# A written order for the early part of a fused attention and MLP kernel, and a later assumed crossbar landing

## Chip, cores and metric

One core of a Trainium2 chip. The metric is the device time of one launch, in microseconds (us). Of the 113 runs of the kernel before beside the experiments, 110 were fast, and 101 of these lie within 0.3% of the median of their rounds; three fell in a slower state (182.75 to 183.62 us, at a granted clock of 0.987 to 0.991), and only fast runs are compared here. A ratio is the mean time of one kernel's fast runs over that of the other's of the same rounds, so it is not quite the ratio of the medians that are quoted beside it.

## The reference

```python
# q, k, v, alpha: (4, 8, 768, 48)  (batch, heads, tokens, head_dim)
for t in range(S):
    state = alpha[:, :, t, :, None] * state + np.einsum('bhd,bhe->bhde', k[:, :, t], v[:, :, t])
    y[:, :, t] = np.einsum('bhd,bhde->bhe', q[:, :, t], state)
x = y.transpose(0, 2, 1, 3).reshape(3072, 384)
h = x @ w_in                                        # (384, 2048)
g = 0.5 * h * (1 + tanh(c * (h + 0.044715 * h**3)))
out = g @ w_out                                     # (2048, 384)
```

## The kernel before

The kernel splits the tokens in six chunks of 128 and each chunk in two pairs of batches: twelve pairs. For a pair it takes logarithms of alpha (`ln`), sums them on TensorE (`cum`, tile `cum`), exponentiates (`b`, `binv`), scales q and k (`qp`, `kp`), transposes them (`t`, tile `qkT`), multiplies and masks them (`attn`, tile `at`; `mask`, tile `atm`), multiplies with v (`y`, tile `yps`), and carries the state (`kv`, `st`). Layer 1 (`l1`, tile `hT`), GELU and layer 2 (`l2`, tile `acc`) follow. Early pairs are transposed on TensorE, the eighth pair and later ones by DMA (ten `DMA_TRANSPOSE` of q and k in the trace, from 97.42 us on), called the crossbar here after the kernel's `xbar`.

The trace shows instructions of an engine in the order in which they are emitted: in that of the changed kernel ScalarE's first 30 instructions, from 0.73 to 20.67 us, stand in the order of its list (`FIRST` below). A scheduler in Python picks that order when the program is built: it plays the tasks through with fixed costs and takes the best candidate at each step. It also puts "idle" products on zeros into gaps of TensorE, to keep the array busy. The parts that matter here, cut:

```python
W = dict(..., landed=2200, xbar_qk=1500, xbar_x=1000, late_x=2500, ..., cold=380, fill=216, zero=1100)

class Scheduler:
    def order(self):
        ...
        while any(left.values()):
            best = None
            for e in LAT:                       # each engine: the ready task that may start first
                ...
            at, e, t = best
            if e == "PE" and self.fill and at < self.until and at - free[e] > 300:
                g = given("ff")
                n = int((at - max(free[e], g if g is not None else at) - 60) * 0.95 // W["fill"])
                if not free[e]:                 # the first gap: the array is slow
                    n = int((at - W["zero"]) // W["cold"])
                if n > 0:
                    ...                         # n idle products
            put(t, at, e)
            ...

    # GpSimd asks for loads in this order; a "gate" is a copy that waits for a tile
    LOADS = ('gatea 0 1', 'v0', 'gateqp 0 1', 'in 0', 'v1', 'in 1', 'in 2', 'in 3', 'out 0', ...)
```

## Time and profile before

| | median us | runs |
|---|---|---|
| before, at the time of the prediction | 180.68 | 3 |
| before, with the runs beside the changed kernel | 180.76 (180.13 to 181.17) | 6 |

The prediction below shows the busy shares, the table by stretch and the waits. What it doesn't show is the start, which turned out to matter. The timeline of TensorE of the kernel before (columns: start, length, engine, line, operation, tiles, shape, count, and in brackets the idle time just before and what ended it):

```profile
1.19 2.74 PE L225 MATMUL idle<-zero 128*128 128x512 bf16 x6 [1.19 <-DVE half L801]
4.33 1.09 PE L282 MATMUL cum<-la,ut_blk 128*128 128x384 f16 x7 [0.40 <-ACT la L295]
5.36 0.82 PE L282 MATMUL cum<-la,ut_blk 128*128 128x384 f16 x7
8.21 0.40 PE L425 MATMUL at<-qkT 64*128 64x128 bf16 x8
17.61 0.40 PE L425 MATMUL at<-qkT 64*128 64x128 bf16 x8
31.82 2.76 PE L527 MATMUL acc<-w_out,gT 128*128 128x384 bf16 x16
```

Six idle products run while alpha is on its way. In the start one idle product takes about 0.43 us (six take 2.74 us here, five take 2.31 in the changed kernel below), twice the 0.22 us of a later one. The first group of seven `cum` products takes 1.09 us and the second, which is the same work, 0.82: the array reaches full speed during the first one (0.82 is also what the groups at 12.24 and 13.37 us take). The two `at` lines are the first attention product of the first and of the second pair; the last line is the start of layer 2.

### The profile page before, as it was taken

How to read it: one execution, taken by the hardware profiler on the slowest of the kernel's cores; microseconds unless marked ns; L12 is line 12 of the kernel's file. 1: busy time of each engine (PE TensorE's matmuls, PEld its weight loads, DVE VectorE, ACT ScalarE, POOL GpSimd, SP SyncE). 2: the span in 40 equal slices, each digit the busy share in tenths (PEclk: the TensorE clock that was granted, in tenths of full speed). 3: DMA queues.
4: the chain of work that ended last, by engine and by line, in shares of the span. 5: the costliest groups of instructions: out<-in, count | busy, mean ns of one | idle time of the engine just before them, and what ended most of it. 6: DMA issues, size and time to landing. Idle time of an engine off the chain costs nothing.

```text
span 178.9 us, 4418 instructions
## 1 busy us (share of the span) xinstructions
PE 171.5 (96%) x1835; PEld 135.0 (75%) x1838; DVE 95.2 (53%) x187; ACT 131.3 (73%) x216; POOL 58.0 (32%) x64
## 2 busy tenths in 40 slices
PE   6979899999999999999999989999999999999992
PEld 2547699666896897797698679688697697786972
DVE  6669751054967894596499779195436405000000
ACT  4669778984898668858788948987988984481831
POOL 2496347986627766566520000000000000000000
PEclk9999999999999999999999999999999999999999
DMA  4999999999999999999998970362270360401102
GB/s 124 269 273 217 208 246 234 229 210 207 227 313 214 221 266 213 185 262 211 201 251 196 159 183 13 68 168 63 44 190 22 88 162 4 117 15 45 47 2 86
DMA packets 48901, 28.86 MB, mean 161 GB/s; under 512 B 37489, under 2 KB 45297, under 8 KB 48881
## 3 DMA queue, kind: packets, MB, share of 16 engines
q0 software_dynamic: 26464, 17.70, 59.5%
q1 hardware_dynamic: 22416, 10.88, 23.8%
q8 instruction: 14, 0.23, 0.6%
q14 instruction: 7, 0.05, 0.1%
HBM read 25.17 MB, written 4.72 MB: 167 GB/s over the span
## 4 chain that ended last, share of the span: by engine, by line
PE 88%; DMA 8%; DVE 1%; ACT 1%; SPq 0%; issue 0%; POOL 0%
PE hT L508 35%; PE acc L527 33%; PE at L425 4%; DMA v<-in_v_dram 3%; PE qkT_ps L364 3%; PE yps L482 3%; DMA qkT<-kp 3%; PE kv L442 2%; PE yps L479 2%; PE cum L314 2%; DMA a<-in_alpha_dram 2%; PE xT_ps L496 1%; PE idle L225 1%; PE cum L282 1%; PE cum L316 1%; PE k_ps L390 1%
## 5 line engine op out<-in xcount | busy, mean ns | idle before, releaser
L527 PE MATMUL acc<-w_out,gT 128*128 128x384 bf16 (+1 forms) x400 | 69.1, 319 | 0.0
L508 PE MATMUL hT<-xT,w_in 128*128 128x256 bf16 x576 | 69.0, 273 | 0.0
L514 ACT ACTIVATE gT<-hT 128x512 bf16<-128x512 f32 x96 | 56.8, 597 | 16.7 <-PE hT L508 13.1
L508 PEld LDWEIGHTS <-w_in 128*128 128x128 bf16 x576 | 61.1, 113 | 1.2
L527 PEld LDWEIGHTS <-gT 128*128 128x128 bf16 x400 | 36.6, 97 | 19.1
L432 DVE TENSOR_TENSOR atm<-at,ut 128x512 bf16<-128x512 f32 x48 | 30.2, 683 | 15.5 <-PE at L425 15.4
L354 DVE TENSOR_TENSOR qp<-q,b 128x768 bf16<-128x768 f32 (+1 forms) x15 | 11.9, 796 | 22.6 <-ACT b L343 14.4
L539 ACT COPY ot<-acc 128x384 f32<-128x384 f32 (+1 forms) x18 | 8.3, 460 | 14.1 <-PE acc L527 11.9
L244 POOL DMA_DIRECT2D k<-in_k_dram x11 | 12.2, 1107 | 8.6 <-DVE stmp L464 3.2
L244 POOL DMA_DIRECT2D q<-in_q_dram x11 | 12.2, 1108 | 7.2 <-DVE qp L354 1.6
L244 POOL DMA_DIRECT2D a<-in_alpha_dram x11 | 12.3, 1114 | 5.4 <-DMA w_in<-in_moe_w_in_dram 1.4
L244 POOL DMA_DIRECT2D vb<-in_v_dram x11 | 12.1, 1103 | 4.5 <-PE hT L508 1.3
L343 ACT ACTIVATE b<-cum 128x768 bf16<-128x768 f32 (+1 forms) x15 | 10.3, 684 | 2.7 <-PE cum L316 1.5
L216 ACT ACT_TABLE_LOAD x9 | 11.5, 1283 | 0.9 <-PEq L832 0.7
L354 DVE TENSOR_TENSOR kp<-k,binv 128x768 bf16<-128x768 f32 (+1 forms) x15 | 11.9, 792 | 0.0
L514 ACT ACT_TABLE_LOAD x9 | 11.5, 1283 | 0.2
L489 DVE CAST x<-yps 128x384 bf16<-128x384 f32 x11 | 6.1, 558 | 8.6 <-PE yps L482 5.6
L343 ACT ACTIVATE binv<-cum 128x768 bf16<-128x768 f32 (+1 forms) x15 | 10.2, 678 | 0.0
L464 DVE TENSOR_TENSOR stmp<-kv,st 128x384 f32<-128x384 f32 x16 | 8.8, 552 | 1.8 <-PE kv L442 1.8
L489 ACT CAST x<-yps 128x384 bf16<-128x384 f32 x13 | 6.2, 476 | 4.8 <-PE yps L482 4.8
L482 PE MATMUL yps<-vb,atm 128*128 128x48 bf16 x192 | 8.7, 183 | 0.8 <-ACT vb L325 0.8
L467 DVE TENSOR_TENSOR st<-stmp,ends 128x384 bf16<-128x384 f32 x16 | 8.9, 558 | 0.6
(63 smaller groups left out, 157.9 us busy)
## 6 DMA issues: line engine op xcount, KB each, us to landing
out_dram<-ot SPq DMA_DIRECT2D x23, 192.0 KB, 3.8
a<-in_alpha_dram POOLq DMA_DIRECT2D x9, 384.0 KB, 11.9
q<-in_q_dram POOLq DMA_DIRECT2D x9, 384.0 KB, 11.5
k<-in_k_dram POOLq DMA_DIRECT2D x9, 384.0 KB, 11.4
vb<-in_v_dram POOLq DMA_DIRECT2D x9, 192.0 KB, 11.6
w_in<-in_moe_w_in_dram POOLq DMA_DIRECT2D x4, 384.0 KB, 10.0
w_out<-in_moe_w_out_dram POOLq DMA_DIRECT2D x4, 384.0 KB, 11.3
a<-in_alpha_dram SPq DMA_DIRECT2D x4, 192.0 KB, 4.1
```

Source lines behind the costliest of these rows:

```text
L216: nc.scalar.add_instruction(mybir.InstLoadActFuncSet(name=nc.get_next_instruction_name(), act_func_set_id=i, engine=mybir.EngineType.Activ ...
L244: dma(u[t][:, lo:hi].rearrange("t b h d -> t (b h) d"), src.rearrange("b h s d -> s (b h) d")[c * C:(c + 1) * C])
L343: self.nc.scalar.activation(u[n].rearrange("t i h d -> t i (h d)")[:, lo:hi], cum, AF.Exp, scale=1.0 if n == "b" else -1.0)
L354: self.nc.vector.tensor_tensor(out, rows, b, op=ALU.mult)
L432: self.nc.vector.tensor_tensor(u["atm", i][:, o], u["at", i][o], self.ut[:, None, :].to_broadcast([self.C, self.H // 2, self.C]), op=ALU.mult)
L464: nc.vector.tensor_tensor(s, acc, old, op=ALU.add)
L467: nc.vector.tensor_tensor(new.rearrange("f p (o d) -> f (p o) d", o=2), acc.rearrange("f p (o d) -> f (p o) d", o=2), ends, op=ALU.mult)
L482: nc.tensor.matmul(y[:, h, :], u["atm", i][:, h % 2, h // 2, :], u["vb"][:, i, h, :], start=c == 0, stop=True, skip_group_check=True)
L489: self.copy(e)(x, u["y", i].rearrange("t h d -> t (h d)"))
L508: self.nc.tensor.matmul(h[:, s], w_in[:, j, nt % 4 + s], self.xT[c % self.NX][:, j, lo:hi].rearrange("p g t -> p (g t)"), start=j == 0, st ...
L514: return lambda e: self.nc.scalar.activation(self.gT[c % self.NG][:, nt:nt + 2, lo * self.C:hi * self.C], f.pop(("h", c, lo, nt)), AF.Gelu ...
L527: self.nc.tensor.matmul(f["acc", c, b][:, lo:hi], self.gT[c % self.NG][:, nt, b * self.C:(b + 1) * self.C], self.w_out[:, nt, lo:hi], star ...
```

## The change

Its intent: the order of every engine in the first 30 us or so is a list found by a search in a replay of the trace, instead of the scheduler's greedy choice; from there on the scheduler goes on as before. A few ordering constraints that had steered the greedy choice are dropped. And the scheduler assumes that the crossbar transposes of the eighth pair land 1.2 us later than it did. The core, cut:

```diff
+COST = {("ACT", "b"): (385, 135), ..., ("DVE", "mask"): (605, 115), ...}      # measured costs, for the written part
@@ Scheduler.order
+        for step in self.first:                 # "engine:task" in the written order; "P:fill.n": n idle products
+            ...
+            go(max(at, free[e] + (W["table"] if t.table not in (None, table) else 0)), e, t)
         while any(left.values()):
             ...
-                if not free[e]:
-                    n = int((at - W["zero"]) // W["cold"])
@@ _Kernel
+    FIRST = """
+        A:table.0 S:load.0 ... A:ln0.0 S:load.5 P:fill.5 P:cum0.0 A:ln0.1 G:gate.0 ... P:cum0.1 A:b0.0 S:load.7
+        A:binv0.0 V:qp0.0 ... P:fill.2 P:t0.0 ... V:qp0.1 P:fill.3
+        P:attn0.0 V:kp0.1 P:t0.2 G:gate.1 S:load.11 G:load.13 ... A:ln1.0 V:mask0.0 P:fill.4
+        P:attn0.1 G:load.15 P:cum1.0 V:mask0.2 A:vb0.0 ... A:ln1.1 V:vb0.1 P:y0.0 ... P:cum1.1 ...
+        (cut) ... P:l20.1 V:ev1.4 P:l20.2 P:kv1.0 P:l20.5
+    """.split()
+    LANDED = {"load.0": 2800, ...}              # landing times of the loads, for the written part
@@ tasks
-            if m == 1:
-                cums[1].deps.append(ys[1, 0])
-                tq = [s.add("turn", ..., xbar=W["xbar_qk"]) ...]
+                tq = [s.add("turn", ..., xbar=W["xbar_qk"], late=W["late_qk"] * (m < 8)) ...]    # late_qk=1200
-                if m in self.NARROW:
-                    vin[j].deps += turned
-                    t.deps += [xts[c, 2 * i], xts[c, 2 * i + 1]]
```

## The prediction

For reading its costs: in the chain of the kernel before, a layer-1 group of six products takes 0.65 to 0.66 us and two idle products at 15.39 us take 0.43; the 1283 ns are ScalarE's load of the GELU table (`ACT_TABLE_LOAD` at 15.78 us; the GELU begins at 17.07).

> **What bounds the kernel now.** I read the page's busy shares and slices first, then the table of engine time by stretch, the waits of TensorE, and the timelines of the two stretches where TensorE was not full.
>
> ```profile
> PE 171.5 (96%) x1835; PEld 135.0 (75%) x1838; DVE 95.2 (53%) x187; ACT 131.3 (73%) x216; POOL 58.0 (32%) x64
> PE   6979899999999999999999989999999999999992
> ```
>
> TensorE is the bound. Its one weak part before the end is the first five slices (22 us), and there is one dent at slice 24. The table by stretch says how much is missing where (columns: stretch, its length, then busy time of PE, PEld, DVE, ACT, POOL with instruction counts, clock, DMA share, GB/s):
>
> ```profile
> 4.30:10.60 6.30, 6.08 (x62) 3.39 (x63) 4.49 (x9) 3.47 (x9) 3.40 (x5) 1.00 0.96 279
> 10.60:31.80 21.20, 19.45 (x236) 16.93 (x237) 12.28 (x26) 17.56 (x34) 13.22 (x18) 1.00 1.18 230
> 31.80:99.00 67.20, 67.20 (x772) 52.88 (x771) 45.96 (x84) 53.32 (x85) 40.21 (x35) 1.00 1.34 226
> 99.00:105.00 6.00, 5.34 (x59) 3.60 (x59) 4.56 (x8) 4.90 (x8) 0.00 (x0) 1.00 0.98 159
> 105.00:175.70 70.70, 70.69 (x714) 57.31 (x708) 25.21 (x41) 49.92 (x79) 0.00 (x0) 1.00 0.29 77
> ```
>
> From 31.8 to 175.7 us TensorE is full but for 0.66 us, so whatever the early part saves is carried to the end unless a load or a crossbar landing newly holds it. Before that, 1.75 us are idle in 10.6 to 31.8. Not all busy time there is work, though: the program has 26 "idle" products (on zeros, to keep the array busy), 6 at the start and 20 later, of which one stands at 46 us. The other 19 fill gaps between 6 and 23 us. The waits of TensorE over the whole run are few:
>
> ```profile
> PE cum L282 <- ACT la L295: 0.9, 2, 0.5
> PE yps L482 <- ACT vb L325: 0.8, 1, 0.8
> PE at L425 <- DMA qkT<-kp: 0.7, 1, 0.7
> PE k_ps L390 <- DVE qkT L382: 0.4, 1, 0.4
> ```
>
> [...] 48 layer-1 products of 256 columns took 5.24 us in the chain, 109 ns each [...]. So one layer-1 group of six products costs 0.655 us and one idle product of 512 columns 0.216 us, and those, not the overlapping durations of the page, are the costs used below. [...] The trace shows 1283 ns, and the first GELU started 0.01 us after the load at 15.78 had ended, so I count 1.28 us[...]. [...]
>
> **The change, part by part.** Useful work is the same. I built both and counted products by output: 128 cum, 112 qkT, 192 at, 272 y, 36 xT, 16 k_ps, 80 kv, 576 hT, 400 acc in both. Only idle products differ, 26 before and 19 after (5 at the start, 13 in the early part, 1 at 46 us). The order of SyncE and GpSimd is the same on both sides, so loads are asked for in the same order. Past the written part the orders agree up to the pair near 100 us.
>
> *Early part, up to the first attention product of the second pair.* Before, ScalarE cast both halves of v (waiting for v until 10.84), then took the second pair's logarithms, then x. After, the logarithm comes ahead of the cast, one cast goes to VectorE, and the second pair's cum stands before the first y. Worked by hand with the durations of the trace: the first half's cum needs its alpha, landed before 10; it starts when the first pair's attention is done, near 10.7, not 12.24; the second half's cum near 11.9, not 13.37; the scaled q and k about 1.5 us sooner; the attention product near 15.5, not 17.61. By itself this would be 2 us.
>
> *But it doesn't all reach the end.* What follows needs loads whose landing this change doesn't move:
>
> ```profile
> 18.86 0.51 ACT L325 CAST vb<-v 128x384 bf16<-128x384 f32 x1
> 22.48 0.56 POOL L261 DMA_DIRECT2D w_out<-in_moe_w_out_dram  x1 [0.99 <-DMA w_in<-in_moe_w_in_dram]
> 23.01 0.82 PE L508 MATMUL hT<-xT,w_in 128*128 128x256 bf16 x6
> ```
>
> The first line is the cast just after the second v landed, near 18.8. The second is GpSimd's issue that waited for the third quarter of w_in, so that quarter was there by 22.4. The third is the first layer-1 group that uses it. Before that group both kernels can do four groups (quarters one and two), and both orders do exactly four. After it both have 12 groups, 7.86 us. Four PSUM banks are cycled there, so the fifth group also needs the first GELU done. In the new order the table load stands after both casts of the second v: v at 18.85, cast 0.35 and latency, y at 19.3, x on ScalarE 19.7 to 20.1, second cast to 20.5, table load 1.28 to 21.8, first GELU to 22.4, fifth group near 22.5. Both bounds agree on 22.5, about 0.5 us sooner than 23.01.
>
> Beside the 12 groups, the old order still had two xT, two k_ps and two kv before its first acc (in the chain 0.17 + 0.45 + 0.34 = 0.96 us). The new one has done most of it: one k_ps (0.23) and one kv (0.17) are left, 0.40. That is 0.56 us more. Sum: 0.5 + 0.56 = about 1.1 us at the start of layer 2 (31.8 becomes 30.7). The balance of TensorE allows it: 1.75 us idle and the six idle products dropped past the start (1.3 us) are what could be saved, 3.05 us at most, and my hand order leaves about 1 us idle near 18.5, while v is awaited, and small gaps besides.
>
> *The eighth pair.* The expected landing of its crossbar transposes is 1.2 us later, so its attention product goes behind two kv units and two more layer-1 groups. Before:
>
> ```profile
> 103.14 0.82 PE L508 MATMUL hT<-xT,w_in 128*128 128x256 bf16 x6
> 104.62 0.62 PE L425 MATMUL at<-qkT 64*128 64x128 bf16 x16 [0.66 <-DMA qkT<-kp]
> 105.18 0.52 PE L442 MATMUL kv<-vb,kp 128*128 128x96 bf16 x8
> ```
>
> TensorE idled 0.66 us. The kv (0.34 us) and two groups (1.31 us), which stood behind the product and need nothing from it, now cover it: the product would come near 105.6, a microsecond after the old landing. VectorE then does the state updates ahead of the masks, which moves the masks some 1.5 us later, but the y of that pair stand behind three more groups, so I expect a wait of 0.1 to 0.2 us there at most. Gain 0.5 to 0.66 us.
>
> Sum: 1.1 + 0.6 = 1.7 us of 180.7, or 0.9%. The tail (175.7 to 178.9 us) and the start (first logarithm at 3.75 us, after its alpha landed) are not touched.
>
> **The rivals.** First: *the replay was not the chip*. A written order is rigid; if one landing (v or a quarter of w_in) comes later than its listed time, TensorE waits with no idle product and nothing else to do, and the early gain shrinks to nothing. For it: in 10.6 to 31.8 the DMA share exceeds 1, [...] and fill work is cut from 19 to 13 in the stretch. Against: the old order was as rigid, and the listed durations agree with the trace (mask 605 + 115 ns against 683 ns measured, and so on). Then only the crossbar part is left: about 180.1 us.
>
> Second: *most of the 3.05 us comes through*. If v lands sooner than I read, or the third quarter of w_in is not what holds the fifth group, the early part alone could give 2.5 us, and the total would be near 177.6. For it: the attention of the second pair is some 2 us earlier. Against: the 22.48 line; work cannot begin before its weights, and 12 groups are 7.86 us whatever the order.
>
> Third: *the gain is given back later*. A TensorE that runs 1 us ahead could meet loads of later pairs that are not in, or find the eighth pair's transposes, queued behind x transposes and stores, later as well. Against: TensorE idles nowhere between 31.8 and 99 us, and the fourth pair's logarithm (39.6), the first that could be held, feeds a cum only at 43.7. In this case time is 179.5 to 180.
>
> **Range and chances.** 80% range: 178.1 (early part 2 us, crossbar in full) to 180.3 (crossbar alone, less a little). Faster by over 2% needs under 177.07 us, which is 3.6 us saved: more than all the early slack that I count. It would take that and the crossbar's 0.66 us together, so 6%. Slower by over 2% has no mechanism here but a state of the chip: 2%. Within 2%: 92%. Runs of before spread over 0.7 us, so the sign should be visible, but not much more.
>
> **What would show each step right or wrong.** Idle products: 19, fewer by seven. The second pair's first attention product near 15.5 (was 17.61). The first group on the third quarter of w_in at 22.3 to 22.7 (was 23.01), started by a GELU's bank or that load; if it starts much earlier, my bound by landing is wrong; if after 23, the replay was. The first acc near 30.5 (was 31.82). About 1 us of idle TensorE near 18 to 19.5, with v as releaser. TensorE full from there to 99 us; if not, the third rival holds. No wait of an attention product on the transposed k near 104; if 0.3 us or more remains, the late landing was set too small. If the time is under 178 or over 180.5, the account of the early part is wrong.

## The result, and the profile after

| | median us | runs | ratio to before, 95% interval |
|---|---|---|---|
| before | 180.76 (180.13 to 181.17) | 6 | |
| changed | 179.66 (179.37 to 179.91) | 6 | 0.994 (0.992 to 0.9961) |

The change gains 1.1 us; 1.7 were predicted, and the time lies inside the range. The busy shares of the changed kernel's page:

```profile
PE 172.0 (97%) x1829; PEld 136.1 (77%) x1831; DVE 95.0 (53%) x187; ACT 130.8 (74%) x216; POOL 58.0 (33%) x64
```

TensorE counts as busier, although it does less. Its table by stretch (the columns of the prediction's table):

```profile
4.30:10.60 6.30, 6.30 (x47) 3.95 (x48) 2.94 (x6) 2.98 (x8) 2.09 (x4) 1.00 0.97 283
10.60:31.80 21.20, 20.58 (x244) 17.59 (x245) 12.41 (x27) 18.77 (x37) 13.56 (x18) 1.00 1.14 219
31.80:99.00 67.20, 67.20 (x780) 53.04 (x779) 46.61 (x87) 52.92 (x85) 41.20 (x36) 1.00 1.37 227
```

The first row is the surprise: TensorE is full from 4.3 to 10.6 us, but finishes 47 products there, against 62 before. It is not idle; it is slow. The clock column says 1.00 in that stretch and doesn't show it; the durations in the timeline of the changed kernel do:

```profile
1.19 2.31 PE L279 MATMUL idle<-zero 128*128 128x512 bf16 x5 [1.19 <-DVE half L853]
4.26 1.44 PE L336 MATMUL cum<-la,ut_blk 128*128 128x384 f16 x7 [0.76 <-DVE ut L864]
5.64 1.44 PE L336 MATMUL cum<-la,ut_blk 128*128 128x384 f16 x7
9.87 0.40 PE L479 MATMUL at<-qkT 64*128 64x128 bf16 x8
16.85 0.40 PE L479 MATMUL at<-qkT 64*128 64x128 bf16 x8
23.16 8.02 PE L562 MATMUL hT<-xT,w_in 128*128 128x256 bf16 x72
31.24 1.46 PE L581 MATMUL acc<-w_out,gT 128*128 128x384 bf16 x8
```

Five idle products stand at the start instead of six, and TensorE then idles 0.76 us instead of 0.40. Both `cum` groups take 1.44 us; the first attention product comes 1.66 us later than before, and the new order has won that back, and 0.76 us more, by the second pair's (16.85 against 17.61). The fifth layer-1 group, for which 22.5 was predicted, begins at 23.16 (before: 23.01), and layer 2 at 31.24 (31.82). At 94 us the same y products stand 0.37 us apart (94.30 before, 93.93 after).

The timeline of the changed kernel at the eighth pair:

```profile
105.18 0.62 PE L479 MATMUL at<-qkT 64*128 64x128 bf16 x16
```

No wait stands before the attention product any more. So the trace of the change is about 0.4 us from the early part, the rest from the crossbar. I had predicted 1.1 and 0.6. What became of the early part?

### The profile page after: what moved, and what is told of

Same layout as the page of the kernel before. It is cut to its first block, busy times and chain, and to the rows that moved or that the text cites. A ratio compares the mean times of both kernels' runs of the same rounds, so it can differ in the third digit from the quotient of the medians.

```text
span 177.8 us, 4409 instructions
## 1 busy us (share of the span) xinstructions
PE 172.0 (97%) x1829; PEld 136.1 (77%) x1831; DVE 95.0 (53%) x187; ACT 130.8 (74%) x216; POOL 58.0 (33%) x64
## 4 chain that ended last, share of the span: by engine, by line
PE 90%; DVE 3%; ACT 3%; issue 1%; POOL 0%; POOLq 0%
PE acc L581 35%; PE hT L562 34%; PE at L479 4%; PE qkT_ps L418 4%; PE yps L536 2%; PE cum L368 2%; PE yps L533 2%; PE kv L496 2%; PE cum L336 2%; PE idle L279 1%; DVE atm L486 1%; ACT qkT L436 1%; PE xT_ps L550 1%; ACT L568 1%; PE cum L370 1%
## 5 line engine op out<-in xcount | busy, mean ns | idle before, releaser
L568 ACT ACTIVATE gT<-hT 128x512 bf16<-128x512 f32 x96 | 56.1, 599 | 15.1 <-PE hT L562 11.6
L397 ACT ACTIVATE b<-cum 128x768 bf16<-128x768 f32 (+1 forms) x15 | 10.2, 683 | 3.1 <-PE cum L340 1.6
L270 ACT ACT_TABLE_LOAD x9 | 11.5, 1283 | 0.9 <-PEq L884 0.7
L568 ACT ACT_TABLE_LOAD x9 | 11.5, 1283 | 0.2
L397 ACT ACTIVATE binv<-cum 128x768 bf16<-128x768 f32 (+1 forms) x15 | 10.2, 681 | 0.0
L543 DVE CAST x<-yps 128x384 bf16<-128x384 f32 x12 | 6.7, 558 | 5.2 <-PE yps L536 5.2
L351 ACT ACTIVATE la<-a 128x768 f16<-128x768 f32 (+1 forms) x11 | 8.5, 783 | 1.1 <-DMA a<-in_alpha_dram 1.0
L436 ACT COPY qkT<-qkT_ps 128x512 bf16<-128x512 bf16 (+1 forms) x9 | 6.5, 728 | 3.6 <-PE qkT_ps L418 3.5
## 6 DMA issues: line engine op xcount, KB each, us to landing
k<-in_k_dram POOLq DMA_DIRECT2D x9, 384.0 KB, 11.8
```

The costliest lines, as they stand in the source:

```text
L270: nc.scalar.add_instruction(mybir.InstLoadActFuncSet(name=nc.get_next_instruction_name(), act_func_set_id=i, engine=mybir.EngineType.Activ ...
L351: self.nc.scalar.activation(u["la"][:, lo:hi, :, 0:self.D], u["a"][:, lo:hi], AF.Ln)
L397: self.nc.scalar.activation(u[n].rearrange("t i h d -> t i (h d)")[:, lo:hi], cum, AF.Exp, scale=1.0 if n == "b" else -1.0)
L568: return lambda e: self.nc.scalar.activation(self.gT[c % self.NG][:, nt:nt + 2, lo * self.C:hi * self.C], f.pop(("h", c, lo, nt)), AF.Gelu ...
```

## The experiments

There were eleven runs, of nine new kernels and two repeats, each with five rounds beside the kernel before. All gave right results.

### The two parts apart, and the start apart

`b_late` is the kernel before with the later landing alone:

```diff
+    late_qk=1200
-                tq = [..., xbar=W["xbar_qk"]) ...]
+                tq = [..., xbar=W["xbar_qk"], late=W["late_qk"] * (m < 8)) ...]
```

> The kernel before, with nothing but the later expected landing of the eighth pair's crossbar transposes; the built order differs from before only near 100 us, where it equals the changed kernel's. My account: the 0.66 us wait of the attention product on the transposed k is gone and the time falls by 0.6 to 0.9 us, to about 180.0 us. Rival (the gain is all the early order's): no change beyond 0.2 us, because a later wait takes its place.

Measured: 180.12 us (before 180.72), ratio 0.9966 (0.9954 to 0.9978), so 0.6 us. The wait on the transposed k is gone from its profile. As expected.

`a_nolate` is the changed kernel with the early order alone:

```diff
-    late_qk=1200
+    late_qk=0
```

> The changed kernel without the later landing: the written early order alone. My account of the result: the early part is worth only about 0.4 us (the traces stand 0.37 us apart at 94 us), so the time is about 180.3 us, and the 0.7 us wait on the transposed k is back. The two parts should add: the falls of this run and of b_late together give the 1.1 us of the whole change. Rival, as I predicted: the early part is worth 1.1 us, about 179.6 us.

Measured: 180.0 us, ratio 0.9956 (0.9942 to 0.9969), which is 0.8 us. The 0.4 us that I expected lies outside its interval (0.56 to 1.05 us), and so does my predicted 1.1. The two parts then add to 1.4 us where the whole gave 1.1; with intervals of 0.2 to 0.4 us on each that is no contradiction, so the early part is worth nearer 0.8 us by this run, and 0.4 in the one pair of traces. Its profiled run fell in the slow state, so I read no waits from it; its first `cum` took 1.44 us as well.

`a_fill6` is the changed kernel with one more idle product:

```diff
-... S:load.5 P:fill.5 P:cum0.0 ...
+... S:load.5 P:fill.6 P:cum0.0 ...
```

> The changed kernel with six idle products at the start, as before, instead of five. In the trace of the changed kernel the first cum of seven products took 1.44 us (1.09 before), and matmuls stayed slow until 9.4 us, and the first attention product came at 9.87 us (8.21 before). Theory: the missing sixth product leaves the array idle too long, so it warms up some 4.5 us later. Then with six: cum back at about 1.1 and 0.8 us, first attention near 8.3, first acc near 30.6 (31.24), time 0.4 to 0.6 us lower, about 179.15. Rival 1 (loads bound): the attention comes sooner but the layer-1 group on the third quarter of w_in stays at 23.1 and the time at 179.66. Rival 2 (chance): the warm-up falls where it will, and the profile shows slow matmuls with six as well.

Measured: 178.34 us (177.96 to 178.79), ratio 0.9865 (0.9839 to 0.989): 2.4 us under before, 1.3 us under the changed kernel, more than twice what I expected. Its timeline:

```profile
1.19 2.74 PE L279 MATMUL idle<-zero 128*128 128x512 bf16 x6 [1.19 <-DVE half L853]
4.34 1.09 PE L336 MATMUL cum<-la,ut_blk 128*128 128x384 f16 x7 [0.41 <-ACT la L349]
8.22 0.40 PE L479 MATMUL at<-qkT 64*128 64x128 bf16 x8
15.36 0.40 PE L479 MATMUL at<-qkT 64*128 64x128 bf16 x8
21.66 8.02 PE L562 MATMUL hT<-xT,w_in 128*128 128x256 bf16 x72
29.74 1.46 PE L581 MATMUL acc<-w_out,gT 128*128 128x384 bf16 x8
```

The start is that of the kernel before, and in this profile the new order keeps all of its lead: the second pair's attention at 15.36, where I had worked out 15.5, and layer 2 at 29.74, 2.1 us before the old kernel's. (The later profiles with a fast start keep less of it, see below.) Rival 1 (loads bound the fifth group) falls with this line: the group was at 21.66, not 23.1. The load itself moved, too. GpSimd asks for w_in behind its second gate, a copy that waits for the second half of the scaled q of the first pair, and that half comes after a `cum`. The gate and the issue that shows the third quarter of w_in landed, in the changed kernel:

```profile
9.81 0.36 POOL L304 CAST gate<-qp 128x1 f32<-128x1 bf16 x1 [3.98 <-DVE qp L408]
23.02 0.56 POOL L315 DMA_DIRECT2D w_out<-in_moe_w_out_dram  x1 [1.06 <-DMA w_in<-in_moe_w_in_dram]
```

and the landing with six idle products, where the gate opened at 8.42:

```profile
21.38 0.56 POOL L315 DMA_DIRECT2D w_out<-in_moe_w_out_dram  x1 [1.01 <-DMA w_in<-in_moe_w_in_dram]
```

In this pair the slow start also asks for weights 1.4 us later, and they land 1.6 us later. That the one follows from the other isn't shown: in `b_fill5`, the next run, the gate opens 1.35 us later than in the kernel before (9.89 against 8.54), and the same quarter is there sooner (by 22.04 us against 22.48).

`b_fill5` is the kernel before with five idle products:

```diff
-                    n = int((at - W["zero"]) // W["cold"])
+                    n = int((at - W["zero"]) // W["cold"]) - 1
```

> The kernel before with five idle products at the start instead of six, nothing else in the order. Theory of the missing sixth product: its cum takes 1.44 us, matmuls stay slow until about 9.4 us, the second pair's attention and the first acc (31.82) come up to 0.5 us later or not at all, as far as v (10.84 us) hides it; time 0 to 0.5 us higher. Rival [...]: matmuls are as fast as before in this profile.

Measured: 180.98 us, ratio 1.0011 (0.9998 to 1.0025). The start is just as slow as the changed kernel's:

```profile
4.33 1.44 PE L282 MATMUL cum<-la,ut_blk 128*128 128x384 f16 x7 [0.83 <-ACT la L295]
10.18 0.40 PE L425 MATMUL at<-qkT 64*128 64x128 bf16 x8
```

Its attention comes 2.0 us later, layer 2 0.75 us later (32.57), and the time is only 0.2 us worse, with an interval of about 0 to 0.45 us. The old order had slack to lose: it waited 0.8 us for v and 0.5 us for alpha near 11 to 12 us anyway, and at the eighth pair its wait on the crossbar shrank from 0.66 to 0.33 us. The changed kernel's profile has neither wait, and the same slow start costs it 1.0 to 1.3 us (the 1.0 comes from `a_fill7` below). That the missing slack is the reason fits the traces and was not tested by itself.

### What keeps the array slow

`a_again` is the changed kernel unaltered (no edit).

> The changed kernel once more, unaltered, beside the kernels with other starts. If the late warm-up belongs to the five idle products, its profile shows again a first cum of 1.44 us and a first attention product near 9.6 to 9.9 us, and the time is 179.7 +- 0.2 us. If it was chance, the profile may show 1.09 us or less, and some of its timed runs should reach the 178.3 us of the kernel with six.

Measured: 179.58 us, ratio 0.9938 (0.9923 to 0.9953); first `cum` 1.44 us, first attention 9.56. The result repeats, and so does the slow start.

`a_fill5_late` keeps five idle products but starts them later, by writing the zeros after the other constants:

```diff
-        nc.vector.memset(self.zero, 0.0)
         nc.vector.memset(self.ones, 1.0)
         ...
             nc.vector.memset(self.half[64 * o:64 * o + 64, o:o + 1], 1.0)
+        nc.vector.memset(self.zero, 0.0)
```

> The changed kernel with its five idle products begun about 0.5 us later (the zeros that they read are written after the other constants), so that they end near 4.0 us, as six do. Theory G (the gap before the first cum, 0.76 us against 0.40, is what keeps the array slow): gap near 0.3 us, first cum about 1.1 us, first attention near 8.3 us, time near 178.4 us. Theory A (the amount of busy time before the first cum decides, 2.3 us against 2.7): still 1.44 us, attention near 9.7 us, time 179.7 us.

Measured: 179.07 us, ratio 0.9913 (0.9895 to 0.9931). Its timeline:

```profile
1.54 2.31 PE L279 MATMUL idle<-zero 128*128 128x512 bf16 x5 [1.54 <-DVE zero L855]
4.26 1.36 PE L336 MATMUL cum<-la,ut_blk 128*128 128x384 f16 x7 [0.40 <-DVE ut L864]
5.56 0.82 PE L336 MATMUL cum<-la,ut_blk 128*128 128x384 f16 x7
8.42 0.40 PE L479 MATMUL at<-qkT 64*128 64x128 bf16 x8
```

The same five products, 0.35 us later, so that the gap is 0.40 us: the array is fast from 5.6 us and the first attention is at 8.42. The profile agrees with the theory of the gap, and not with that of the amount; it is one profile. Half of the loss is back in the time. Why only half, the cast of the first v on ScalarE suggests, here and in `a_fill6`:

```profile
11.64 0.51 ACT L379 CAST vb<-v 128x384 bf16<-128x384 f32 x1 [0.90 <-DMA v<-in_v_dram]
```

```profile
10.63 0.51 ACT L379 CAST vb<-v 128x384 bf16<-128x384 f32 x1 [0.20 <-DMA v<-in_v_dram]
```

In this profile, with a fast start, the first v is what comes last. It landed a microsecond later here, everything behind its cast moved, and the second pair's attention came at 16.29, not 15.36. The chain that ended last runs through this load in `a_fill5_late`, in `a_fill7` and in `a_fill6_vb`, as it does in the kernel before; how the landing fell in the runs without a profile is not known.

`a_fill7` has seven idle products:

```diff
-... S:load.5 P:fill.5 P:cum0.0 ...
+... S:load.5 P:fill.7 P:cum0.0 ...
```

> The changed kernel with seven idle products: the seventh should end near 4.36 us, just when the first logarithm lets the cum begin. Either theory: the array is warm no later than with six; the first cum takes 0.85 to 1.1 us; first attention near 8.1 to 8.3 us; time within 0.2 us of 178.34 us. If the seventh delays the cum by 0.2 us or more, that much slower.

Measured: 178.56 us, ratio 0.9882 (0.9861 to 0.9903); no idle time before the first `cum`, which took 0.91 us; attention at 8.31. As expected: no better and no worse than six within the spread. This is the comparison on one chip and in the same rounds as `a_again`: 1.0 us for two idle products.

`a_fill6_again` is `a_fill6` once more (no further edit).

> The kernel with six idle products once more, unaltered, to see how often six leave the array fast in time: first cum about 1.1 us or less and first attention near 8.2 us if it is warm early (as in its first profile), up to 8.7 us otherwise. Time 178.2 to 178.7 us, and below the changed kernel's 179.6 us either way.

Measured: 178.74 us, ratio 0.9884 (0.9846 to 0.9923). This time the array was late even with six:

```profile
4.29 1.44 PE L336 MATMUL cum<-la,ut_blk 128*128 128x384 f16 x7 [0.35 <-DVE ut L864]
5.67 1.37 PE L336 MATMUL cum<-la,ut_blk 128*128 128x384 f16 x7
8.70 0.40 PE L479 MATMUL at<-qkT 64*128 64x128 bf16 x8
```

It got fast near 6.8 us, not 4.8, and the attention came at 8.70 (the second pair's at 16.09). So chance plays a part in when, but hardly in the main difference: five profiles of kernels with five products and the wide gap (`after`, `a_again`, `a_nolate`, `b_fill5`, `a_gate0`) were all slow until 8.6 us or later; eight with a gap of at most 0.43 us (`before`, `b_late` and the other kernels with six, seven or the later five) were fast by 4.5 to 6.8 us. Three of these thirteen profiles fell in slow runs, which differ from the others later in the kernel; in the start they agree with their group.

### Two attempts to do better

`a_fill6_vb` has six idle products and casts the second half of the second v on VectorE, ahead of the masks, so that ScalarE loads the GELU table sooner:

```diff
-... P:fill.5 P:cum0.0 ...  V:vb1.0 G:load.28 V:mask1.2 ...  V:mask1.3 A:vb1.1 P:kv0.0 ...
+... P:fill.6 P:cum0.0 ...  V:vb1.0 V:vb1.1 G:load.28 V:mask1.2 ...  V:mask1.3 P:kv0.0 ...
```

> Six idle products, and the cast of the second v's second half on VectorE instead of ScalarE, where it stands ahead of the GELU table load. With six alone the fifth layer-1 group began at 21.66 us, on the bank that the first GELU freed, and TensorE idled only about 0.3 us there. My theory (the chain v, x, cast, table load, GELU sets it): table load near 19.25 instead of 19.72, first GELU near 20.55, fifth group near 21.4, held next by the third quarter of w_in, there by 21.38; time 0.2 to 0.3 us lower, about 178.1. Rival: VectorE's masks, 0.35 us later, hold y by as much, and nothing is gained.

Measured: 178.85 us, ratio 0.989 (0.9866 to 0.9914). Not better than six alone, and not tellable from it. Its profile had the late start (first `cum` 1.44 us), and its first v landed at 11.8 us, so its times cannot be laid beside the first profile of `a_fill6`; from the second pair's second attention product to the fifth group it took 3.93 us against 4.10, so the step itself may have given 0.17 us there. Whether it is worth anything stays open.

`a_gate0` and `a_fill6_gate0` open GpSimd's second gate with the first half of the scaled q, with five and with six idle products, so that loads are asked for 2 to 3 us sooner:

```diff
-    LOADS = ('gatea 0 1', 'v0', 'gateqp 0 1', 'in 0', ...)
+    LOADS = ('gatea 0 1', 'v0', 'gateqp 0 0', 'in 0', ...)
-... V:qp0.0 A:bend0.0 ...  P:t0.2 G:gate.1 S:load.11 ...
+... V:qp0.0 G:gate.1 A:bend0.0 ...  P:t0.2 S:load.11 ...
```

> The changed kernel (five idle products) with GpSimd's second gate opened by the first half of the scaled q instead of the second, so that w_in and the second v are asked for near 7.3 us instead of 10.28. It separates the two ways in which a slow start can reach the end. Theory E (it goes through the engines: attention, evictions, masks, the second y): loads are there sooner, but the second pair's attention stays near 16.8 and 19.0 us, the fifth layer-1 group near 23.0, time 179.4 to 179.7 us. Theory L (through the gated loads): v and the third quarter of w_in land 1 to 2 us sooner, the fifth group comes near 22, time near 178.7 us. If instead the earlier loads crowd out the q and k of the second pair, the first attention of that pair is later and the time is above 179.8 us.

> Six idle products and the earlier gate. With six alone the second v landed just before 17.4 us and its cast followed at 17.65 us, and the second half of that pair's y with it; the fifth group was at 21.66 us. If v is what holds that chain, it may begin up to 0.5 us sooner, no more, because the masks of that pair end near 17.1 us and the evictions fill ScalarE: time 177.9 to 178.3 us. If the loads crowd out the second pair's q and k (landing by 13 us now), the gain turns into a loss: above 178.6 us.

Measured: `a_gate0` 181.06 us in the median, 11 of 23 runs slow; `a_fill6_gate0` 182.86 us, 17 of 22 runs slow, while in the same rounds one of 43 runs of the kernel before was. The fast runs have ratios of 0.9951 (0.9922 to 0.998) and 0.9985 (0.9959 to 1.0011), so with six products even the fast ones lose nearly all of the gain. Both profiles fell in slow runs and are not used as a cause. What follows is only that the gate should stay where it is. Which way the slow start reaches the end, through the engines or through the gated loads, these two could not tell apart. The profiles of the changed kernel (`after` and `a_again`) speak for the engines: from 7 to 23 us the chain that ended last runs through attention, masks, evictions and the GELU, with no load in it.

The best kernel of the study is `a_fill6`, with `a_fill7` its equal: 178.3 to 178.7 us, ahead of both kernels compared.

## Why the prediction was right or wrong

- *TensorE full after 31.8 us, so an early gain is carried.* Right: 67.20 of 67.20 us in the changed kernel, and in `a_fill6` a lead of 2.0 us at the same work (the first `cum` of the third pair at 32.51 us against 34.51) is still 2.0 us at 94 us (92.31 against 94.30).
- *Idle products 26 to 19.* The count was right, and what it meant was missed. The step that failed is the half sentence "the start (...) not touched": one of the seven dropped products stood in the start. I counted it as free; taking it away leaves the array at half speed for four to five microseconds more (in the chains, the second `cum` group takes 1.30 us in the changed kernel, and the same work at 13.53 us in the kernel before takes 0.66). In the first pair of profiles that is the whole difference from my working: with the product put back, the attention is at 15.36 (I said 15.5), without it at 16.85. In the other profiles with a fast start it is not the whole: the attention is at 15.73 in `a_fill7`, 16.09 in `a_fill6_again`, 16.29 in `a_fill5_late` and 16.42 in `a_fill6_vb`. In three of these four it waited, through the cast, for the first v (landed at 11.1 to 11.8 us), in the fourth the array got fast late (near 6.8 us). My working took the landing of that v as given.
- *Fifth layer-1 group near 22.5, 0.5 us sooner.* Wrong for the changed kernel: 23.16, 0.15 us later. With the start restored it came at 22.11 to 22.59 in the four profiles just named, which is what I had said, and at 21.66 in the first of `a_fill6`. The chain I named is the one that holds in the changed kernel; the chain of work that ended last, in order of time, runs through it link by link:

```profile
19.82 0.58 ACT kn L451
20.41 0.38 ACT x L543
20.79 0.41 ACT vb L379
21.22 1.28 ACT L568
23.16 8.02 PE hT L562 x72
```

  Each link took what I had given it, but x waited behind an eviction (`kn`) that the late attention product had pushed to 19.82, so all of it is 0.7 us later than worked out.
- *Loads "whose landing this change doesn't move".* Wrong. The third quarter of w_in was there by 22.48 us before, 23.02 after and 21.38 with six products. The gate before it follows the scaled q, but by `b_fill5` it doesn't set the landing alone, so the cause stays open. Nor was this load what held the fifth group: in the chains of `after`, `a_again` and `a_fill6` the group follows the GELU. In the changed kernel the two were close (load there by 23.02, GELU done at 23.12). So my bound by landing, which I used against the second rival, was not the one that held. That rival (the early part alone gives 2.5 us, total near 177.6, 3.1 us less) still goes too far: with six or seven products the whole gain is 2.1 to 2.4 us (178.34 to 178.74), between my 1.7 and its 3.1.
- *0.56 us of other work moved ahead of the twelve groups.* Right: they took from 23.16 to 31.02 us, and k_ps and kv after them 0.39 us (0.40 said). So the early sum was -0.15 + 0.56 = 0.4 (the traces show 0.5 at the third pair's first `cum`, 0.4 at 94 us) instead of 0.5 + 0.56 = 1.1; the first term alone was off. Layer 2 began at 31.24, where the prediction has 30.7 in its sum and 30.5 in its list of signs.
- *Crossbar 0.5 to 0.66 us.* Right: 0.6 us by `b_late`, the wait gone, the product at 105.18.
- *About 1 us of idle TensorE while v is awaited.* Wrong: 0.62 us in the whole stretch. The second v landed within 7.6 us of its issue instead of 8.8, and TensorE was late enough not to wait for it.
- *First rival, the replay was not the chip.* True in its kind, not in its place. No listed load was late; the start was, and the list of costs has one cost for a product, whatever the array's speed. The third rival did not show: TensorE full to 99 us, no DMA among its waits.

That the time came as near as it did is partly luck, because two errors were opposite: an order better than I worked out (with the start restored the third pair's first `cum` is 1.3 to 2.0 us early in the two profiles of `a_fill6` and 1.6 in `a_fill7`, not 1.1), and a start that takes 1.0 to 1.3 us away.

On the array's speed the traces show this. An idle product took 0.43 us in the start and 0.22 later. Idle products from 1.19 us (1.54 in `a_fill5_late`) with a gap of at most 0.43 us before the first `cum` gave full speed at 4.5 to 4.8 us in five profiles of eight, and at 5.4 to 6.8 in the other three; with a gap of 0.75 to 0.83 us it came only 4 to 6 us after work had resumed at 4.3, at 8.6 to 10.2 us, in five profiles of five. That it is the gap which keeps the array slow is my reading of `a_fill5_late` against `a_again`, where nothing but the gap and the start of the products differ; what sets the moment is not in the trace.

## What to carry to other kernels

Filler work at the start is not free slack: here TensorE was fast by 4.5 to 6.8 us where filler ran to within 0.43 us of the first real product, and slow until 8.6 us or later where it ended 0.75 to 0.83 us before. Let it run until the first real product, and check the length of the first few products, not only their idle time. A cost list with one duration per operation cannot price this, so an order found in a replay should be rerun with the fillers restored. And slack that hides a fault in one order can be gone in a tighter one: the same missing product cost the old kernel about 0.2 us and the new one 1.0 to 1.3. Once the start was mended, the landing of the first v held the new order in three profiles of five: look for what comes last after each repair.

## What else the traces show

- The moment at which the array gets fast varies from run to run: the same kernel (`a_fill6`) was fast near 4.8 us in one profile and near 6.8 in another.
- The profile's column of the granted clock reads 1.00 in 4.3 to 10.6 us of the changed kernel while a group of products took up to 1.8 times as long (1.44 us against 0.82). Only durations show the slow start.
- The load of the GELU table took 1283 ns, and nothing more showed as time of its own: in the changed kernel the GELU began at 22.51 us, after a load from 21.22 that took 1.28, and the cast before the load had ended at 21.20.
- The landing of one load moves from run to run. The first v landed 6.2 us after its issue in the kernel before and 6.8 in `a_fill5_late`; the second v landed 8.8 us after its issue in the kernel before and 7.5 us after it in `a_fill6`, with nearly the same time of issue (9.75 and 9.63 us). The runs do not show why.
